# Two column pairs of a token-mixing MLP's first product as blocks of seven products, and weight sums over four steps

## The chip, the core and the metric

The kernel runs on one core of a Trainium2 chip. TensorE (PE) multiplies, with its weight loads (PEld) beside it; VectorE (DVE), ScalarE (ACT) and GpSimd (POOL) work on tiles in SBUF and on TensorE's results in PSUM; SyncE (SP) issues most of the transfers, POOL and ACT a few. All times are device microseconds. The time of the kernel is the median of several executions; the profile comes from one execution of its own.

## The reference

One sequence of 2048 tokens with 512 channels passes through a linear attention block and a token-mixing MLP, both with a residual:

```python
h  = x + A(layernorm(x), wqkv, w_phi, wo)      # linear attention, 32 heads of 16
h2 = h + B(layernorm(h), w1, b1, w2, b2)

def B(x, w1, b1, w2, b2):
    h = layernorm(x)                               # [S=2048, D=512]
    u = gelu(einsum("bsd,sf->bdf", h, w1) + b1)    # contracts the 2048 tokens, F=1792
    y = einsum("bdf,fs->bds", u, w2) + b2          # contracts F, back to 2048 tokens
    return y transposed to (tokens, channels)
```

All in float32. The change concerns B alone: its first product (w1 transposed times h) and its second (w2 transposed times u).

## The kernel before

**Arithmetic.** Each float32 operand is split into a hi part (a cast by ACT, rounded to TensorE's fast float32 format) and a lo part (the difference, by DVE or POOL); a product is the sum of three: hi·hi, hi·lo, lo·hi (`mm3`, L64 to L68; `split`, L59 to L62).

**Token loop.** After the attention's preparation (to about 136 us) a loop over `it` runs 18 times over the 16 token tiles: numerator, output projection (`s_wo`), residual `s_h` (DVE L634, with SP's store of h L635), the two layer norms' moments (`s_moments`, ACT) and `s_hn`, which leaves the normalized tile as hi and lo (`HN`, "hs"); its lo part is POOL's. The order of instructions on TensorE, DVE, ACT and POOL is written out by hand here (`manual_schedule`); SP's is left to the scheduler.

**First product.** u has 14 tiles of 128 rows (F) by 512 columns (D), taken in 7 column pairs p (`NP`). A pair sums over 16 token tiles; each contributes 2 × 3 plain products of 128×128 by 128×512 (`fill`, `mm3`: the tile name is "pu"). Pairs 0 and 1 are woven into the token loop, as the tiles appear; the others follow it. `stream` (L672 to L679) loads the weights of two token tiles by two F tiles (256 KB) and splits them: hi on ACT (L663), lo on DVE (L670). After a pair comes `gelu` (ACT, L797), which puts both tiles of u into one 128×1024 tile.

**Second product.** y has 16 tiles of tokens, taken as 8 pairs `sp`; each sums over the 7 pairs p of u: 56 steps (sp, p). A step multiplies a 2×2 block of w2 (two F tiles by two token tiles) with a 2×2 block of u (two F tiles by two halves of D, 256 columns each) in seven products instead of eight (the Strassen scheme in Winograd's form). The operands are sums of blocks: of the weights, four sums on DVE over the data of two steps at once (`w2_sums`, L848, operations of 128×256 at L854 to L857), then the seven operands are split for two steps at once (`w2_parts`, L865, 128×1792, ACT and DVE, both at L875); of u, four sums and splits once per pair (`operands_u`, L800). In `pair_of_tiles` (L933) products 1 and 6 run as `narrow` (L908): three products of 256 columns (L913). Products 2, 3, 4, 5 and 7 run as `wide` (L916): one product of 512 columns, hi·hi and hi·lo side by side (L921), and one of 256 columns for lo·hi (L924); the halves are added when the bank is read. The last pair of token tiles runs all seven as narrow, and its last three steps together: 147 products in a row. When a pair of token tiles is complete, DVE and ACT combine the banks (L972) and POOL issues three stores of 256 KB that accumulate onto h in `out` (L991, and L992 for "low"). The order is held by `in_order` (L839).

Of the kernel before, what the change touches and what calls it, by code (L numbers as in the profile page):

```python
# [31 lines left out]
LAG = 3  # L32
WARM = 10
# [4 lines left out]
def block_kernel(ctx: ExitStack, tc: tile.TileContext, x, xT, wT, phic, wo, w1, b1, w2, b2,  # L38
# [34 lines left out]
    wqp = aq.enter_context(tc.tile_pool(name="wqp", bufs=1, side="right"))  # L73
    wqh = wqp.tile([P, KD, D], F32R, name="wqh")
    wql = wqp.tile([P, KD, D], F32R, name="wql")
    kvB = wqp.tile([P, 2, P], F32, name="kvB")
    kvS = wqp.tile([P, 4, 64], F32, name="kvS")
    sums = wqp.tile([P, SUMS, NPR, 2, 2], F32, name="smq")
    wqp.tile([P, 504], F32, name="pad")
# [378 lines left out]
    ms.enter_context(tc.manual_schedule(engines={ET.PE, ET.DVE, ET.Activation, ET.Pool}))  # L458
# [112 lines left out]
    ps_f = ctx.enter_context(tc.tile_pool(name="ps_f", bufs=2, space=PSUM, reuse_waits="tile"))  # L571
    wst = ExitStack()
# [5 lines left out]
    HN, HT, PHT, OS, PO, VE = {}, {}, {}, {}, {}, {}  # L578
# [68 lines left out]
    def s_hn(t):  # L647
        hn = ak.tile([P, D], F32, name="hn")
# [23 lines left out]
    def stream(src, k0, n, c0, w):  # L672

        raw = wf.tile([P, n, w], F32, name="wraw")
        wh_ = wf.tile([P, n, w], F32R, name="whi")
        wl_ = wf.tile([P, n, w], F32R, name="wlo")
# [44 lines left out]

    for it in range(NT + 2):
# [23 lines left out]
        if it + 3 < NT:  # L746
            s_ez(it + 3)
        if 0 <= it - 2 < NT:
            s_hn(it - 2)
# [10 lines left out]
        if 0 <= it - 1 < NT:  # L760
            s_wo(it - 1)
        for w in work[1:]:
            w()
        if 0 <= it - 1 < NT:
            s_h(it - 1)
        flush(1)
    flush()
    ms.close()
    a2.close()
    aq.close()  # L770

    NP = NF // 2
    HD = D // 2
    up = ctx.enter_context(tc.tile_pool(name="up", bufs=1, side="right", reuse_waits="tile"))
    uo = ctx.enter_context(tc.tile_pool(name="uo", bufs=2, side="right", reuse_waits="tile"))
    ws = ctx.enter_context(tc.tile_pool(name="ws", bufs=2, side="right", reuse_waits="tile"))
    ur = ctx.enter_context(tc.tile_pool(name="ur", bufs=4, side="right", reuse_waits="tile"))
    ut = ctx.enter_context(tc.tile_pool(name="ut", bufs=1, side="right", reuse_waits="tile"))
    ps_b = ctx.enter_context(tc.tile_pool(name="ps_b", bufs=4, space=PSUM, reuse_waits="tile"))
    NEAR = 2
    near = [up.tile([P, 7, 2, HD], F32R, name=f"un{p}") for p in range(NEAR)]  # L790
    up.tile([P, 120], F32, name="pad")
    U, UB, far = {}, {}, {}
# [7 lines left out]
    def operands_u(p):  # L800
        u = U[p]
        tt = ut.tile([P, 3, HD], F32, name="tt")
        e = nc.gpsimd if p < NEAR else nc.vector
        e.tensor_sub(tt[:, 0], u[:, 0], u[:, 1])
        e.tensor_sub(u[:, 0], u[:, 2], u[:, 0])
        e.tensor_sub(tt[:, 1], u[:, 2], tt[:, 0])
        e.tensor_sub(tt[:, 2], u[:, 3], tt[:, 1])
        if p < NEAR:
            for n0, src in ((0, u), (4, tt)):
                o = near[p][:, n0:n0 + src.shape[1]]  # L810
                split(o[:, :, 0], o[:, :, 1], src, nc.vector)
            for m in range(7):
                UB[p, m] = near[p][:, m]
            return
        for m in range(7):
            at = (p - NEAR) * 7 + m
            if at % 2 == 0:
                far[at // 2] = big.tile([P, 2, 2, HD], F32R, name="uf", tag="big")
            UB[p, m] = far[at // 2][:, at % 2]
            split(UB[p, m][:, 0], UB[p, m][:, 1], u[:, m] if m < 4 else tt[:, m - 4], nc.vector)  # L820

    for p in range(NP):
        while FN[p] < NT:
            fill(p, ps_b)
        for c in range(2):
            gelu(2 * p + c, PU[p][c])
        if p < NEAR:
            operands_u(p)
    for p in range(NEAR, NP):
        operands_u(p)  # L830
    wst.close()
    hp = ctx.enter_context(tc.tile_pool(name="hp", bufs=1, reuse_waits="tile"))

    STEPS = [(sp, p) for sp in range(NT // 2) for p in range(NP)]
    GRP = 2
    AW, RAW = {}, {}
    QUEUE = {}

    def in_order(*ops):  # L839

        for op in ops:
            with ExitStack() as st:
                for ins in QUEUE.values():
                    st.enter_context(tc.issue_after(ins))
                ins = op().ins
            QUEUE[ins.engine] = ins

    def w2_sums(g):  # L848
        other = g > AHEAD + 2 and g % 4 == 1
        raw = RAW[g] = (hp if other else ws).tile([P, GRP, 7, P], F32, name="wraw", bufs=1 if other else 3)  # L850
        for i, (sp, p) in enumerate(STEPS[g * GRP:(g + 1) * GRP]):
            nc.sync.dma_start(raw[:, i, 0:4].rearrange("p (k i) s -> p k (i s)", k=2),
                              w2v[:, 2 * p:2 * p + 2, sp * 2 * P:(sp + 1) * 2 * P])
        sums = (lambda: nc.vector.tensor_add(raw[:, :, 4], raw[:, :, 0], raw[:, :, 2]),  # L854
                lambda: nc.vector.tensor_sub(raw[:, :, 5], raw[:, :, 4], raw[:, :, 1]),
                lambda: nc.vector.tensor_sub(raw[:, :, 0], raw[:, :, 1], raw[:, :, 0]),
                lambda: nc.vector.tensor_sub(raw[:, :, 6], raw[:, :, 3], raw[:, :, 5]))  # L857
        if g < AHEAD:
            with tc.issue_after(LO[-18]):
                for op in sums:  # L860
                    op()
        else:
            in_order(*sums)

    def w2_parts(g):  # L865
        home = hp if g % 3 == 2 else ws
        wh_ = home.tile([P, GRP, 7, P], F32R, name="whi")
        wl_ = home.tile([P, GRP, 7, P], F32R, name="wlo")
        for i, step in enumerate(STEPS[g * GRP:(g + 1) * GRP]):
            AW[step] = wh_[:, i], wl_[:, i]  # L870
        raw = RAW.pop(g)
        if g < AHEAD:
            split(wh_, wl_, raw, nc.vector)
        else:
            in_order(lambda: nc.scalar.activation(wh_, raw, AF.Copy), lambda: nc.vector.tensor_sub(wl_, raw, wh_))  # L875

    AHEAD = 2
    for g in range(AHEAD):
        w2_sums(g)
        w2_parts(g)  # L880
    for g in range(AHEAD, AHEAD + 2):
        w2_sums(g)
    parts_next, sums_next = [], []

    def stream_w2(n):

        if (n + 1) % NP == 0:
            for g in sums_next:
                w2_sums(g)
            sums_next.clear()  # L890
        if n % GRP == 0:
            parts_next.append(n // GRP + AHEAD)
        if (n + 2) % NP == 0:
            return
        for g in parts_next:
            if g * GRP < len(STEPS):
                w2_parts(g)
            if (g + 2) * GRP < len(STEPS):
                if (n + 3) % NP == 0:
                    sums_next.append(g + 2)  # L900
                else:
                    w2_sums(g + 2)
        parts_next.clear()


    P1, P2, P3, P4, P5, P6, P7 = (1, 1), (3, 3), (6, 2), (2, 6), (4, 4), (5, 5), (0, 0)

    def narrow(o, ps, m, sp, opens, closes):  # L908

        for p in ps:  # L910
            wh_, wl_ = AW[sp, p]
            for i, (x, y) in enumerate(((wh_, 0), (wh_, 1), (wl_, 0))):
                in_order(lambda: nc.tensor.matmul(o, x[:, m[0]], UB[p, m[1]][:, y], start=opens and p == 0 and i == 0,  # L913
                                                  stop=closes and p == NP - 1 and i == 2, skip_group_check=True))

    def wide(sp, p, *products):  # L916


        wh_, wl_ = AW[sp, p]
# [13 lines left out]
    def pair_of_tiles(sp, p):  # L933
# [6 lines left out]
        if t + 2 == NT:  # L940
            if p < NP - 3 or end:
# [3 lines left out]
                for o, m, opens in places if end else places[5:] + places[:5]:  # L945
                    narrow(o, ps, m, sp, opens, True)
                if end:
                    last_sums(t, HB)
# [126 lines left out]
```

## Time and profile before

| | us |
|---|---|
| median of 3 runs | 519.57 (519.33 to 519.91) |
| span of the profiled execution | 517.9 |
| TensorE busy in it | 513.2 |
| DVE, ACT, POOL busy | 395.0, 285.3, 235.9 |

The profiled execution has no time of its own beside its span; the 1.7 us between span and median are what lies around the span. By stages, from the trace's start: attention's preparation 0 to 136, token loop to 260, the five remaining column pairs to 375.5, the first seven pairs of token tiles of the second product to 496.8, the last pair with the final sums and stores to the end.

A line of a group reads: source line, engine, operation, result<-operands, shape, count | busy us, mean ns | idle time of the engine before them, and what ended it. A matmul's record has a modelled end; the distance between two starts is what one costs.

### The profile page before, as it was taken

How to read it: one execution, taken by the hardware profiler on the slowest of the kernel's cores; microseconds unless marked ns; L12 is line 12 of the kernel's file. 1: busy time of each engine (PE TensorE's matmuls, PEld its weight loads, DVE VectorE, ACT ScalarE, POOL GpSimd, SP SyncE). 2: the span in 40 equal slices, each digit the busy share in tenths (PEclk: the TensorE clock that was granted, in tenths of full speed). 3: DMA queues.
4: the chain of work that ended last, by engine and by line, in shares of the span. 5: the costliest groups of instructions: out<-in, count | busy, mean ns of one | idle time of the engine just before them, and what ended most of it. 6: DMA issues, size and time to landing. Idle time of an engine off the chain costs nothing.

```text
span 517.9 us, 9772 instructions
## 1 busy us (share of the span) xinstructions
PE 513.2 (99%) x3761; PEld 434.0 (84%) x3761; DVE 395.0 (76%) x719; ACT 285.3 (55%) x501; POOL 235.9 (46%) x182
## 2 busy tenths in 40 slices
PE   9999999999999999999999999999999999999997
PEld 8888888888887777777788888888899999999997
DVE  6799889989987899697336624625797899888993
ACT  6999853526267877767756423425464434433530
POOL 3579997876999999974224000000001102110210
PEclk9999999999999999999999999999999999999999
DMA  8642301021302334333255433532134586557732
GB/s 311 209 142 84 102 22 42 1 83 44 122 27 97 103 103 119 107 103 123 82 163 162 123 94 90 184 102 62 41 115 94 141 201 136 139 156 181 137 48 61
DMA packets 46493, 57.66 MB, mean 111 GB/s; under 512 B 4080, under 2 KB 33136, under 8 KB 46448
## 3 DMA queue, kind: packets, MB, share of 16 engines
q1 hardware_dynamic: 43136, 51.38, 31.4%
q0 software_dynamic: 3024, 5.51, 7.6%
q8 instruction: 29, 0.48, 0.4%
q10 hardware_dynamic: 288, 0.17, 0.1%
q14 instruction: 16, 0.13, 0.1%
HBM read 46.81 MB, written 10.22 MB: 110 GB/s over the span
## 4 chain that ended last, share of the span: by engine, by line
PE 97%; DVE 1%; ACT 1%; issue 0%; DVEq 0%
PE pu L66 13%; PE pu L68 12%; PE pu L67 12%; PE py L921 11%; PE py L913 10%; PE py L924 6%; PE po L66 3%; PE pk_ps L66 3%; PE po L68 3%; PE po L67 3%; PE pk_ps L67 3%; PE pk_ps L68 3%; PE pv L67 3%; PE pv L66 3%; PE pv L68 3%; PE tr L591 2%
## 5 line engine op out<-in xcount | busy, mean ns | idle before, releaser
L991 POOL DMA_DIRECT2D out<-ot x14 | 12.5, 941 | 170.3 <-DVE ot L972 170.3
L66 PE MATMUL pu<-hs,whi 128*128 128x512 f32 x224 | 87.7, 394 | 0.0
L67 PE MATMUL pu<-hs,whi 128*128 128x512 f32 x224 | 87.2, 389 | 0.0
L68 PE MATMUL pu<-hs,wlo 128*128 128x512 f32 x224 | 86.5, 389 | 0.0
L670 DVE TENSOR_TENSOR wlo<-wraw,whi 128x512 fp32r<-128x512 f32 x56 | 46.9, 841 | 46.5 <-ACT whi L663 46.2
L875 ACT ACTIVATE whi<-wraw 128x1792 fp32r<-128x1792 f32 x26 | 44.0, 1704 | 30.9 <-issue 17.4
L663 ACT ACTIVATE whi<-wraw 128x512 fp32r<-128x512 f32 x56 | 34.6, 625 | 44.4 <-PE pu L67 39.4
L875 DVE TENSOR_TENSOR wlo<-wraw,whi 128x1792 fp32r<-128x1792 f32 x26 | 52.4, 2019 | 0.0
L66 PEld LDWEIGHTS pu<-hs,whi 128*128 128x128 f32 x224 | 42.0, 188 | 9.1 <-ACT hj L641 0.2
L68 PEld LDWEIGHTS pu<-hs,wlo 128*128 128x128 f32 x224 | 42.0, 188 | 8.9
L67 PEld LDWEIGHTS pu<-hs,whi 128*128 128x128 f32 x224 | 42.1, 188 | 8.5
L921 PE MATMUL py<-uf,whi 128*128 128x512 f32 x175 | 48.4, 395 | 0.0
L484 POOL TENSOR_TENSOR ez<-eq,zB 128x1024 f32<-128x1024 f32 x16 | 38.4, 2405 | 3.8 <-ACT zB L544 3.8
L913 PE MATMUL py<-uf,whi 128*128 128x256 f32 x210 | 39.0, 283 | 0.0
L213 POOL TENSOR_TENSOR pk<-pk,sk 128x1024 f32<-128x1024 f32 x16 | 31.1, 1949 | 11.2 <-DVE sk L212 10.0
L508 POOL TENSOR_TENSOR eq<-eq,w 128x1024 f32<-128x1024 f32 x16 | 32.4, 2026 | 3.2 <-DVE w L505 3.2
L921 PEld LDWEIGHTS py<-uf,whi 128*128 128x128 f32 x175 | 30.1, 189 | 3.9
L913 PEld LDWEIGHTS py<-uf,whi 128*128 128x128 f32 x210 | 32.8, 192 | 0.0
L217 POOL TENSOR_TENSOR zacc<-zacc,pk 128x1024 f32<-128x1024 f32 x13 | 31.4, 2412 | 0.5
L924 PEld LDWEIGHTS py<-uf,wlo 128*128 128x128 f32 x175 | 27.1, 189 | 3.8
L913 PE MATMUL py<-uf,wlo 128*128 128x256 f32 x105 | 29.7, 283 | 0.0
L924 PE MATMUL py<-uf,wlo 128*128 128x256 f32 x175 | 28.7, 281 | 0.0
(200 smaller groups left out, 1303.9 us busy)
## 6 DMA issues: line engine op xcount, KB each, us to landing
wraw<-in_w SPq DMA_DIRECT2D x112, 256.0 KB, 3.0
xraw<-in_xT SPq DMA_DIRECT2D x16, 256.0 KB, 2.9
xh<-in_x SPq DMA_DIRECT2D x16, 256.0 KB, 2.6
h<-in_x SPq DMA_DIRECT2D x16, 256.0 KB, 2.7
out<-h SPq DMA_DIRECT2D x16, 256.0 KB, 2.1
out<-ot POOLq DMA_DIRECT2D x14, 256.0 KB, 4.4
wraw<-in_wT SPq DMA_DIRECT2D x12, 256.0 KB, 5.1
out<-low POOLq DMA_DIRECT2D x7, 256.0 KB, 4.2
```

What stands on the lines that cost most here:

```text
L66: nc.tensor.matmul(o, ah, bh, start=first, stop=False)
L67: nc.tensor.matmul(o, ah, bl, start=False, stop=False)
L68: return nc.tensor.matmul(o, al, bh, start=False, stop=last).ins
L217: nc.gpsimd.tensor_add(zacc, zacc, PK[t])
L484: nc.gpsimd.tensor_mul(EZ[t], EQ[t], zB)
L508: nc.gpsimd.tensor_mul(heads(EQ[t]), heads(EQ[t]), W[t].rearrange("p g c h -> p (g c h)").unsqueeze(2).to_broadcast([P, 2 * H, DH]))
L663: nc.scalar.activation(wh_, raw, AF.Copy)
L670: LO.append(nc.vector.tensor_sub(wl_, raw, wh_).ins)
L875: in_order(lambda: nc.scalar.activation(wh_, raw, AF.Copy), lambda: nc.vector.tensor_sub(wl_, raw, wh_))
L913: in_order(lambda: nc.tensor.matmul(o, x[:, m[0]], UB[p, m[1]][:, y], start=opens and p == 0 and i == 0, stop=closes and p == NP - 1 and i ...
L921: in_order(lambda: nc.tensor.matmul(o, wh_[:, m[0]], UB[p, m[1]], start=p == 0, stop=False, skip_group_check=True))
L924: in_order(lambda: nc.tensor.matmul(o[:, 0], wl_[:, m[0]], UB[p, m[1]][:, 0], start=False, stop=p == NP - 1, skip_group_check=True))
```

## The change

- **Kinds of column pairs.** Pairs 0 and 1 stay plain, inside the token loop. The other five follow `KINDS = "vuuvv"`: pair 2 plain ("v"), pairs 3 and 4 as blocks ("u"), pairs 5 and 6 plain. Their work is cut into 8 steps for each pair (a step takes two token tiles), numbered 0 to 39; the 56 steps of the second product follow as 40 to 95.
- **Block steps of the first product.** A "u" step multiplies a 2×2 block of w1 (two token tiles by two F tiles) with a 2×2 block of h (two token tiles by two halves of D) in seven products, all narrow: 21 products of 256 columns for 12 of 512. After eight steps `u_out` combines the four banks (one ACT and five DVE operations), and `u_gelu` applies gelu two steps later.
- **Operands of h.** For this the normalized float32 tiles are kept (`HF`). For each of eight pairs of token tiles four sums (`h_ops`, DVE, 128×256) and one split (`h_parts`, 128×1024) are made once and used by both block pairs. Sums of pairs 0 to 6 stand in the token loop from `it` 14 on or between the first steps, those of pair 7 behind step 3's weight parts.
- **Weights of the block steps.** SP loads 256 KB as before and one more tile of 64 KB; then POOL issues a transfer of 128 KB that adds onto the loaded tiles in SBUF (`add_raw`). Two sums by DVE for two steps remain (`w_sums`).
- **Weights of the second product.** `w_sums` makes the four sums for four steps at a time (128×512 for each operation); the splits (`w_parts`) go one step at a time (128×896, or 128×512 for a plain step) into a ring of three buffers, and for the later steps three places out of six in the pool `big`.
- **Second product.** Product 7 runs narrow in place of wide: 4 wide and 3 narrow products in a step. The signs in the combination change, and a pair of token tiles has four stores (128 KB and three of 256 KB).
- **Order.** `manual_schedule` takes SP in as well and holds to the end of the kernel; `in_order` is gone. The lo parts of the last two normalized tiles go from POOL to DVE. A Gelu on a small tile stands in iteration 10 of the token loop, and with it the table load that the first Gelu brings.

```diff
+PLAIN = 2
+KINDS = "vuuvv"
...
-    ms.enter_context(tc.manual_schedule(engines={ET.PE, ET.DVE, ET.Activation, ET.Pool}))
+    ms.enter_context(tc.manual_schedule(engines={ET.PE, ET.DVE, ET.Activation, ET.Pool, ET.SP}))
...
-        split(HN[t][:, 0], HN[t][:, 1], hn, nc.gpsimd)
+        if t < NT - 2:
+            split(HN[t][:, 0], HN[t][:, 1], hn, nc.gpsimd)
+        else:
+            nc.scalar.activation(HN[t][:, 0], hn, AF.Copy)
+            DL.append(lambda: nc.vector.tensor_sub(HN[t][:, 1], hn, HN[t][:, 0]))
...
+    def block_ops(e, v, t0, t1, t2):
+        return [lambda: e.tensor_sub(t0, v[0], v[1]), lambda: e.tensor_sub(v[0], v[2], v[0]),
+                lambda: e.tensor_sub(t1, v[2], t0), lambda: e.tensor_sub(t2, v[3], t1)]
...
+    def load_raw(g):
...
+        for k in range(2):
+            src, r, c = blocks(2 * g + k)
+            nc.sync.dma_start(RAW[g][:, k, 1:5].rearrange("p (k i) s -> p k (i s)", k=2),
+                              src[:, r:r + 2, c:c + 2 * P])
+            if STEPS[2 * g][0] == "u":
+                nc.sync.dma_start(RAW[g][:, k, 0], src[:, r + 1, c:c + P])
...
+    def add_raw(g):
...
+            nc.gpsimd.dma_start(RAW[g][:, k, 0:2].rearrange("p i s -> p (i s)"), src[:, r, c:c + 2 * P],
+                                accum_op=ALU.add)
...
+    def w_sums(g):
...
+        plain = STEPS[2 * g][0] == "y"
+        raw = BLOCK[g // 2 % 2] if plain else RAW[g]
+        if plain:
+            nc.vector.tensor_add(raw[:, :, 0], raw[:, :, 3], raw[:, :, 1])
+        nc.vector.tensor_add(raw[:, :, 5], raw[:, :, 0], raw[:, :, 2])
+        nc.vector.tensor_add(raw[:, :, 6], raw[:, :, 4], raw[:, :, 5])
+        if plain:
+            nc.vector.tensor_add(raw[:, :, 1], raw[:, :, 1], raw[:, :, 2])
+    def w_parts(n):
...
+        if n >= Y0 and (n - Y0) % 6 < 3:
+            PARTS[n] = [big.tile([P, 7, P], F32R, name="wp", tag="big") for _ in range(2)]
+        else:
+            t = ws[n % 3].tile([P, 2, 7, P], F32R, name="wp")
+            PARTS[n] = t[:, 0], t[:, 1]
+        k = slice(1, 5) if STEPS[n][0] == "v" else slice(0, 7)
+        split(PARTS[n][0][:, k], PARTS[n][1][:, k], RAW[n // 2][:, n % 2, k], nc.vector)
...
+    def h_parts(j):
+        h_sums(j)
+        v = HF.pop(j).rearrange("p i (k d) -> p (i k) d", k=2)
+        split(CB[j][:, :, 0], CB[j][:, :, 1], v, nc.vector)
...
+        if it == 10:
+            nc.scalar.activation(mhalf[:, 1:2], mhalf[:, 2:3], AF.Gelu_apprx_tanh)
...
+        some(DQ, {14: 6, 15: 6}.get(it, 0))
         if 0 <= it - 1 < NT:
             s_h(it - 1)
         flush(1)
+        some(DQ, {14: 4}.get(it, 0))
...
+    def products(n, banks, x, first, last):
+        a, b, c, d = banks
+        for o, m, opens in ((a[:, 0], P1, True), (a[:, 1], P6, False), (d[:, 0], P7, True), (b[:, 0], P5, True),
+                            (b[:, 1], P4, False), (c[:, 0], P3, True), (c[:, 1], P2, False)):
+            narrow(o, n, m, x(m[1]), first and opens, last)
...
-        w3, w2, w7, w5, w4 = (b3, P3), (b2, P2), (b7, P7), (b5, P5), (b4, P4)
...
+        w3, w2, w5, w4 = (b3, P3), (b2, P2), (b5, P5), (b4, P4)
+        if first:
+            ws_(w3, w2)
+        elif not end:
+            ws_(w3, w2, w5, w4)
+        narrow(b16[:, 0], n, P1, x(1), first, end)
+        narrow(b16[:, 1], n, P6, x(5), False, end)
+        narrow(b7[:, 0], n, P7, x(0), first, end)
...
+        if kind == "u":
+            if j == 0:
+                BANKS[0] = four_banks(i % 2)
+            products(n, BANKS[0], lambda m: NB[j][m], j == 0, j == NT // 2 - 1)
+            if j == NT // 2 - 1:
+                b = list(BANKS[0])
+                later(0, lambda: u_out(i, b))
+                later(2, lambda: u_gelu(i))
...
+    for j, n in enumerate((0, 1, 2, 3, 5, 8, 10), 1):
+        at(n - 1.5 if j > 3 else n - 0.5, h_sums, j)
+        at(n, h_parts, j)
```

More of the change, by code (lines that the diff above doesn't have):

```diff
@@ L766, in block_kernel @@
         flush(1)
-    flush()
[L768 to L792, printed above, removed]
+        some(DQ, {14: 4}.get(it, 0))
+        if it == 13:
+            for j in range(6):
+                DQ.extend(h_ops(j, nc.vector))
+        if it in (14, 15):
+            add_raw(it - 14)
+        if it == 16:
+            DQ.extend(h_ops(6, nc.vector))
+    some(DL)
+    flush()
+    U, UB, UT, SPARE = {}, {}, {}, []
     def gelu(f, pu):
@@ L822, in block_kernel @@
[L822 to L861, printed above, removed]
-        else:
-            in_order(*sums)
@@ L865, in w2_parts @@
[L865 to L875, printed above, removed]
@@ L906, in block_kernel, with u_sums @@
[L906 to L919, printed above, removed]
+    def u_sums(p):
+        u, tt = U[p], hp.tile([P, 3, HD], F32, name="tt")
+        UT[p] = tt
+        for op in block_ops(nc.vector, [u[:, k] for k in range(4)], tt[:, 0], tt[:, 1], tt[:, 2]):
+            op()
@@ new lines, in block_kernel, with narrow @@
+    for p in range(PLAIN):
+        while FN[p] < NT - 1:
+            fill(p)
+    a2.close()
+    cbb = ctx.enter_context(tc.tile_pool(name="cbb", bufs=1, side="right", reuse_waits="tile"))
+    ps_b = ctx.enter_context(tc.tile_pool(name="ps_b", bufs=4, space=PSUM, reuse_waits="tile"))
+    CB[4] = cb_tile(4)
+    P1, P2, P3, P4, P5, P6, P7 = (2, 1), (4, 3), (6, 2), (3, 6), (0, 4), (5, 5), (1, 0)
+    def narrow(o, n, m, x, opens, closes):
+        wh_, wl_ = PARTS[n]
+        for i, (w, y) in enumerate(((wh_, 0), (wh_, 1), (wl_, 0))):
+            nc.tensor.matmul(o, w[:, m[0]], x[:, y], start=opens and i == 0, stop=closes and i == 2, skip_group_check=True)
@@ L994, in last_h @@
+        if end:
+            last_sums(t, HB)
+        return []
     def last_h(t):
@@ new lines, in block_kernel @@
+    at(len(STEPS) - 18, last_h, NT - 2)
+    at(len(STEPS) - 12, last_b, NT - 2)
+    HB = []
+    load_raw(2)
+    load_raw(3)
+    load_raw(4)
+    add_raw(2)
+    step(0)
+    step(1)
+    for p in range(PLAIN):
+        fill(p)
+    step(2)
+    wst.close()
+    hp = ctx.enter_context(tc.tile_pool(name="hp", bufs=1, reuse_waits="tile"))
+    for j in range(5, NT // 2):
+        CB[j] = cb_tile(j)
+    w_parts(3)
+    load_raw(5)
+    add_raw(4)
+    made = 4
+    DQ.extend(h_ops(7, nc.vector))
@@ new lines, in block_kernel, with prepare @@
+    made = set(range(made))
+    def prepare(m):
+        if m >= len(STEPS):
+            return
+        w_parts(m)
+        made.add(m)
+        if m >= Y0:
+            if m % 4 == (2 if m > Y0 + 3 else 3):
+                w_sums(m // 4 * 2 + 2)
+        elif m % 2 == 0 and m + 2 < Y0:
+            w_sums(m // 2 + 1)
+        if m ^ 1 in made:
+            load_raw(m // 2 + 4)
+            if 2 * (m // 2 + 3) < len(STEPS):
+                add_raw(m // 2 + 3)
+    for n in range(0, len(STEPS)):
+        now[0] = n
+        ready = len(STORES)
+        if n > 2:
+            step(n)
+        if ready:
+            store()
+        for f in PENDING.pop(n - 0.5, []):
+            f()
+        if n == Y0 - 5:
+            w_sums(Y0 // 2)
+        if n + 2 < Y0 and n + 2 not in made:
+            prepare(n + 2)
+        if n + 5 >= Y0 and (n < Y0 or STEPS[n][2] != NP - 2):
+            if n > Y0 and STEPS[n][2] == NP - 1:
+                prepare(n + 4)
+            prepare(n + 5)
+        for f in PENDING.pop(n, []):
+            f()
@@ L1030, in _layout @@
+    assert not STORES
+    ms.close()
 def _layout(A_x, A_wqkv, A_w_phi, A_wo, B_w1, B_b1, B_w2, B_b2):
```

345 lines of the change are left out of this document (212 added, 133 removed).

## The prediction

> **What bounds the kernel now.** I read the busy shares first, then the chain, TensorE's waits, and only then the stages that the change touches.
>
> ```profile
> span 517.9 us, 9772 instructions
> PE 513.2 (99%) x3761; PEld 434.0 (84%) x3761; DVE 395.0 (76%) x719; ACT 285.3 (55%) x501; POOL 235.9 (46%) x182
> PEclk9999999999999999999999999999999999999999
> PE 97%; DVE 1%; ACT 1%; issue 0%; DVEq 0%
> ```
>
> TensorE is busy 99% of the span, 97% of the chain that ended last is its own work, and its granted clock is full in every slice. Its waits with a named releaser:
>
> ```profile
> PE pk_ps L352 <- DVE eps L57: 1.1, 1, 1.1
> PE pn L609 <- DVE h L634: 0.2, 1, 0.2
> ```
>
> There are 1.3 us in all, both ahead of the changed stages. So the time is a count of products times their spacing, and the other engines matter only where the change makes one of them late. The span lacks 1.7 us of the 519.57 us median; I add these to whatever span comes out.
>
> **Price of each product.** A record's duration is modelled (0.39 us), so I take distances between starts.
>
> ```profile
> 259.95 0.39 PE L66 MATMUL pu<-hs,whi 128*128 128x512 f32 x1
> ...
> 359.91 0.39 PE L66 MATMUL pu<-hs,whi 128*128 128x512 f32 x1
> ...
> 365.35 0.39 PE L66 MATMUL pu<-hs,whi 128*128 128x512 f32 x1
> ...
> 375.55 0.61 PE L921 MATMUL py<-un,whi 128*128 128x512 f32 x2
> ```
>
> The 24 products between 359.91 and 365.35 take 0.2267 us each. The 510 issued from 259.95 to 375.55 give the same 0.2267, so that whole stage has no stall.
>
> ```profile
> 379.91 0.72 PE py L913 x6
> 380.63 1.16 PE py L921 x5
> 381.79 0.59 PE py L924 x5
> 382.38 0.72 PE py L913 x6
> ...
> 496.79 17.65 PE py L913 x147
> ```
>
> In these pieces of the chain (start, length, product count) a 256-column product costs 17.65/147 = 0.120, a wide one 1.16/5 = 0.232, its 256-column low part 0.59/5 = 0.118.
>
> **TensorE's sum.** Pairs 3 and 4 lose 2 × 96 = 192 plain products: −192 × 0.2267 = −43.5 us. They become 2 × 8 steps × 21 narrow products: 336 × 0.120 = +40.3. Per pair that is 20.2 us instead of 21.8: seven eighths of the columns, at 3% more per column. In 49 steps of the second product, product 7 goes from wide plus low to three narrow ones: 3 × 0.120 − 0.232 − 0.118 = +0.01 each, +0.5. Net −2.7 us. The narrow spacing comes from a stretch of 147 in a row with the same operand shapes, each with its own weight load, so I take it unchanged (the bound above it is a rival below).
>
> The Trainium skill, "TensorE: Matmul & The Clock Gate", section "Back-to-back issue gap", would turn the sign: it gives about 131 ns for a sustained 512-column product and N/2.4 + 2.5 ns, 109 ns, for 256 columns alone. By these the sum would be −25 + 37, a loss of about 11 us. The rows above disagree by 96 ns in the wide case and decide.
>
> **DVE, the engine that must keep up.** The new work is in 128-row operations, priced by these groups (last figures: busy us, mean ns, then idle before):
>
> ```profile
> L62 DVE TENSOR_TENSOR uf<-u,uf 128x256 fp32r<-128x256 f32 x20 | 7.7, 419 | 0.3 <-ACT uf L61 0.3
> L62 DVE TENSOR_TENSOR un<-tt,un 128x768 fp32r<-128x768 f32 x2 | 1.9, 950 | 0.0
> L62 DVE TENSOR_TENSOR un<-u,un 128x1024 fp32r<-128x1024 f32 x2 | 2.7, 1340 | 2.5 <-ACT un L61 2.5
> L855 DVE TENSOR_TENSOR wraw<-wraw 128x256 f32<-128x256 f32 x28 | 11.9, 424 | 0.8
> L875 DVE TENSOR_TENSOR wlo<-wraw,whi 128x1792 fp32r<-128x1792 f32 x26 | 52.4, 2019 | 0.0
> 247.36 0.69 DVE L670 TENSOR_TENSOR wlo<-wraw,whi 128x512 fp32r<-128x512 f32 x1
> ```
>
> Thus 0.42 for 256 columns, 0.69 for 512, and on straight lines between neighbours 1.09 for 896 and 1.22 for 1024 (1.34 by the row, which I take as the upper end).
>
> The second product's weight work is not on the path. Per pair of token tiles DVE spends now 3.5 × (2.02 + 4 × 0.42) = 13.0 us on it, afterwards 7 × 1.09 + 1.75 × 4 × 0.69 = 12.5, in a TensorE time of 7 × 2.48 = 17.4. No wait of TensorE there ends with DVE before, so the sums over four steps are worth nothing; if DVE alone set the pace they would be worth at most 7 × 0.5 = 3.5 us. ACT's seven casts of 0.95 (896 columns, between its rows below) for 3.5 of 1.70 and POOL's fourth store per pair of tiles have room in the same 17.4 us, ACT being busy 52.30 of 121.30 us:
>
> ```profile
> 375.50:496.80 121.30, 121.30 (x787) 110.52 (x787) 108.74 (x192) 52.30 (x60) 15.88 (x18) 1.00 0.59 139
> ```
>
> In the token loop, iterations 14 and 15 get 16 of the h-block sums (0.42 each, 6.7 us).
>
> ```profile
> 241.10:248.00 6.90, 6.90 (x74) 5.40 (x74) 3.40 (x5) 5.04 (x12) 3.23 (x3) 1.00 0.24 76
> 248.00:254.90 6.90, 6.90 (x73) 5.39 (x72) 1.91 (x5) 4.96 (x12) 1.85 (x2) 1.00 0.24 78
> 254.90:261.70 6.80, 6.80 (x59) 5.29 (x59) 2.31 (x6) 4.90 (x11) 1.85 (x2) 1.00 0.24 77
> 240.16 1.94 POOL L508 TENSOR_TENSOR eq<-eq,w 128x1024 f32<-128x1024 f32 x1 [0.48 <-DVE w L505]
> 240.53 2.11 DVE L670 TENSOR_TENSOR wlo<-wraw,whi 128x512 fp32r<-128x512 f32 x1
> ```
>
> The windows list (after the length) busy us of TensorE, weight loads, DVE, ACT and POOL: DVE has 13.0 us free of 20.6. But a two-input DVE operation that meets POOL work lasts until POOL ends: 2.11 instead of 0.69. "SBUF — State Buffer", section "Who interferes with whom", in the Trainium skill explains it by an exclusive lock on shared ports; these two rows agree. What could be late is the h tile that TensorE transposes next. I allow 0 to 0.3 us.
>
> In iteration 16 the low parts of the plain fills' last weights, of steps 0 and 1 and of tile 14 (until now POOL's) stand in one DVE queue. ACT's part of it now:
>
> ```profile
> 257.67 0.63 ACT L61 ACTIVATE hs<-hn 128x512 fp32r<-128x512 f32 x1
> 258.21 0.62 ACT L663 ACTIVATE whi<-wraw 128x512 fp32r<-128x512 f32 x1
> ```
>
> Adding the two new casts of 0.62 and four low parts of 0.69, with DVE following ACT, the last low part ends near 261.4. TensorE wants it after six plain products from 259.95, at 261.5. Spare 0.1, so 0 to 0.5 us. Tile 15's low part, next in that queue, is wanted some 2 us after it can be there.
>
> The narrowest place is the first block pair. The part buffers are three deep, so the hi cast of step 10 waits for the end of step 7. Counted from the end of step 6: 2.72 (step 7, 12 × 0.2267) + 2 × 0.69 (pair 2's gelus ahead in ACT's queue) + 0.95 (hi, 896 columns) + 1.09 (lo) = 6.14. DVE then has, in order, two weight sums (0.84), one h part (1.22), the last four h sums (1.68) and step 11's lo (1.09): 10.97. TensorE wants that lo after 2.72 + 3 × 2.52 + 2 × 0.12 = 10.52. Late 0.45, and 0.57 at 1.34 per h part. Step 12 has no h sums ahead; the lag is not repeated. The ACT prices are:
>
> ```profile
> L875 ACT ACTIVATE whi<-wraw 128x1792 fp32r<-128x1792 f32 x26 | 44.0, 1704 | 30.9 <-issue 17.4 <-PE py L913 8.7 <-DVE wraw L857 4.8
> L797 ACT ACTIVATE u<-pu,b1s 128x512 f32<-128x512 f32 x14 | 9.5, 687 | 10.0 <-PE pu L68 9.9
> L797 ACT ACT_TABLE_LOAD x1 | 1.3, 1283 | 0.0
> 247.48 0.20 ACT L640 ACTIVATE ve<-ve 128x1 f32<-128x1 f32 x1 [1.73 <-DVE h L634]
> ```
>
> The Gelu table load, moved into the token loop, fits ACT's 1.73 us gap there: nothing; without that gap up to 1.28.
>
> Together 0 to 1.4 us of new stall, and no gain below that, as no stall stands there before. I take 0.5: the one place where the rows say late.
>
> **Transfers.**
>
> ```profile
> q1 hardware_dynamic: 43136, 51.38, 31.4%
> q0 software_dynamic: 3024, 5.51, 7.6%
> wraw<-in_w SPq DMA_DIRECT2D x112, 256.0 KB, 3.0
> out<-ot POOLq DMA_DIRECT2D x14, 256.0 KB, 4.4
> L991 POOL DMA_DIRECT2D out<-ot x14 | 12.5, 941 | 170.3 <-DVE ot L972 170.3
> ```
>
> Each block step loads 256 + 64 KB and accumulates 128 KB into them through POOL. Queue time per MB is 0.314 × 517.9/51.38 = 3.17 us, and for the 21 accumulating stores 0.076 × 517.9/21 = 1.87 us each, half for 128 KB. So a step needs 1.04 + 0.94 = 1.98 us of 2.52. Step 3 starts at 259.95 + (30 + 36) × 0.2267 = 274.9; the first accumulate is issued about then and lands (4.4 by the row) near 279.5, DVE wants it near 280; later ones are issued four steps, 10 us, ahead of their sums. Cost nothing; POOL's 0.94 us per issue hides in its idle time. As an accumulation into SBUF is not in this trace, its other end is a rival below. SP's order is now fixed too: a weight load stands behind a store of h that waits for DVE. Such a load is wanted an iteration (6.9 us) on and lands in 3.0: nothing, without that lead 3.0 once.
>
> **Forecast:** 519.57 − 2.7 + 0.5 = 517.4 us, alone 516.5 to 518.5 (no stall, less a little, to 1.6 us of it).
>
> **Rivals.**
>
> *DVE is late through the whole first block pair* (chance 0.15). From step 3's lo to step 11's, DVE has 5 × 0.69 + 4 × 1.09 + 6 × 1.22 + 12 × 0.42 + 6 × 0.42 = 22.7 us against TensorE's 5 × 2.72 + 3 × 2.52 = 21.2. For it: strided 256-column operands and POOL meetings have no row here; a fifth more is 4.5 us. Against it: DVE is through with the token loop some 7 us before step 3, though three buffers let it keep only two steps (5 us) of any lead. Of 1.5 + 4.5 us that leaves 1 to 3 us in place of the 0.5: 518.0 to 520.0, mostly no change to tell.
>
> *The accumulating loads pace the blocks* (0.11, the slower side). If their queue time is 2.5 times the row's, 0.94 → 2.35, a step takes 3.4 us: 16 × 0.87 = 14 us more, of which the 10 us between issue and sums absorb most: +4, 521 us. It decides from about 2.2 times the row, or a landing over some 13 us. For it: such a transfer reads SBUF back, unlike any load here, and POOL issues it. Against: the stores in the trace accumulate too, at 4.4 us.
>
> *The narrow products are paced by their weight loads* (0.02).
>
> ```profile
> L913 PEld LDWEIGHTS py<-uf,whi 128*128 128x128 f32 x210 | 32.8, 192 | 0.0
> ```
>
> A load lasts 0.192 us; if the loads did not overlap as they do at 0.120, 336 × 0.072 = 24 us come on top: 541. From 0.128 on the gain is gone. The page's 109 ns for 256 columns beside 131 for 512 belongs here; by its figures alone the time would be some 531.
>
> *A wait in a shared queue that I have not placed* (0.06), such as the token loop's stores ahead of SP's loads: 520 to 523.
>
> **How the numbers follow.** The forecast's case has 0.66. About 0.2%, 1 us, can be told from no change. Faster (below 518.5) takes the forecast's case and 0.02 of DVE's lateness: 0.68. Same: the other 0.13 and 0.02 of the last rival: 0.15. Slower: 0.11 + 0.02 + 0.04 = 0.17. The range begins at 516.5 (without stall 516.9, less 0.4 for spacing) and reaches to 520.0, past DVE's lateness; 0.18 or so lies outside.
>
> **What would show it.** Right: TensorE with 168 narrow products in each of two block pairs lasting 20.2 us; a stage sum 3.2 us shorter; new waits below 1.4 us, the largest on a step's lo around step 11. The first rival shows as a row of waits of narrow products for DVE over steps 9 to 15; the second as DVE weight sums waiting for POOL's transfers; the third as spacing above 0.12. Wrong in general: a wait of TensorE over 1 us anywhere from 185 us on, or a granted clock below 1.00.

## The result, and the profile after

The changed kernel takes 516.49 us (median of 4 runs, 516.23 to 517.07), the one before 519.61 (4 runs, 519.33 to 519.91): a ratio of 0.9941, 95% interval 0.9927 to 0.9955. It is 3.1 us faster where 2.2 were forecast, and 0.01 us below the lower end of the range (516.5). The page of the changed kernel, with the lines that answer to those of before:

```profile
span 514.5 us, 10292 instructions
PE 509.4 (99%) x3954; PEld 439.7 (85%) x3954; DVE 432.5 (84%) x736; ACT 300.7 (58%) x530; POOL 247.1 (48%) x195
PEclk9999999999999999999999999999999999999999
q1 hardware_dynamic: 45440, 52.43, 32.6%
q0 software_dynamic: 6336, 8.52, 12.1%
PE 95%; DVE 2%; ACT 1%; issue 0%; DVEq 0%
wraw<-in_w POOLq DMA_DIRECT2D x16, 128.0 KB, 3.9
```

TensorE is the bound as before: fewer busy us with 193 more recorded products, at a full clock. DVE has 37.5 us more to do and is still not on the path. TensorE's waits:

```profile
PE pk_ps L358 <- DVE eps L62: 1.1, 1, 1.1
PE pn L616 <- DVE h L641: 0.2, 1, 0.2
PE pu L336 <- POOL ph L361: 0.2, 1, 0.2
```

The third line is new, but this wait lies in the first 10 us, far ahead of the change. No wait stands in the first or second product. The marks between the stages, from TensorE's timeline of the changed kernel (start, length, line):

```profile
288.23 0.28 PE L951 MATMUL py<-hs,wp 128*128 128x256 f32 x1
...
328.55 0.40 PE L71 MATMUL pu<-hs,wp 128*128 128x512 f32 x1
...
372.09 0.39 PE L958 MATMUL py<-cb,wp 128*128 128x512 f32 x1
...
493.19 0.28 PE L951 MATMUL py<-cb,wp 128*128 128x256 f32 x1
```

The block pairs take 328.55 − 288.23 = 40.32 us for 336 narrow products: 0.1200 each. The second product's first 49 steps take 493.19 − 372.09 = 121.10; read at the same places before they take 121.08.

To see where a span differs I cut each trace at four products: the 41st, the last of the output projection, the first of the second product, the first of the last 147. The differences of their starts, in us, for the profiled executions of all kernels below:

| kernel | to the 41st | token loop | first product | second product | rest | span |
|---|---|---|---|---|---|---|
| before | 7.92 | 251.80 | 115.83 | 121.08 | 21.29 | 517.91 |
| after | 7.41 | 252.01 | 112.67 | 121.10 | 21.26 | 514.45 |
| x1_plain | 7.59 | 252.13 | 115.83 | 121.10 | 21.25 | 517.91 |
| x2_sums_late | 8.23 | 252.03 | 115.23 | 121.52 | 21.46 | 518.46 |
| x3_dve_sums | 7.47 | 252.04 | 113.31 | 121.10 | 21.25 | 515.17 |
| x4_two_steps | 7.46 | 252.04 | 112.71 | 121.10 | 21.25 | 514.55 |
| x5_three | 7.88 | 251.96 | 114.09 | 127.43 | 21.55 | 522.90 |
| x6_pool_lo | 7.69 | 252.02 | 112.65 | 121.10 | 21.26 | 514.71 |
| x7_table | 7.47 | 251.80 | 112.67 | 121.81 | 21.56 | 515.31 |
| x7_again | 7.77 | 251.79 | 112.65 | 121.10 | 21.26 | 514.58 |
| x8_sums_ahead | 7.61 | 252.01 | 112.66 | 121.10 | 21.25 | 514.63 |
| x9_seven_wide | 7.50 | 252.49 | 112.66 | 121.32 | 21.27 | 515.24 |
| c0_after | 8.48 | 252.02 | 112.70 | 121.68 | 21.26 | 516.13 |

Between before and after, 3.16 of the 3.46 us come from the first product. 0.51 more come from the start, which varies between executions (the rows of after and c0_after, 7.41 and 8.48, are the same kernel), and 0.21 are lost in the token loop.

### The profile page after: what moved, and what is told of

Same layout as the page of the kernel before. It is cut to its first block, busy times and chain, and to the rows that moved or that the text cites. A ratio compares the mean times of both kernels' runs of the same rounds, so it can differ in the third digit from the quotient of the medians.

```text
span 514.5 us, 10292 instructions
## 1 busy us (share of the span) xinstructions
PE 509.4 (99%) x3954; PEld 439.7 (85%) x3954; DVE 432.5 (84%) x736; ACT 300.7 (58%) x530; POOL 247.1 (48%) x195
## 3 DMA queue, kind: packets, MB, share of 16 engines
q0 software_dynamic: 6336, 8.52, 12.1%
## 4 chain that ended last, share of the span: by engine, by line
PE 95%; DVE 2%; ACT 1%; issue 0%; DVEq 0%
PE py L951 22%; PE pu L71 10%; PE pu L72 9%; PE pu L73 9%; PE py L958 9%; PE py L960 4%; PE pk_ps L71 3%; PE pk_ps L72 3%; PE pk_ps L73 3%; PE pv L73 3%; PE pv L72 3%; PE pv L71 3%; PE po L71 3%; PE po L73 2%; PE po L72 2%; PE pn L616 2%
## 5 line engine op out<-in xcount | busy, mean ns | idle before, releaser
L66 ACT ACTIVATE wp<-wraw 128x896 fp32r<-128x896 f32 (+1 forms) x96 | 79.8, 869 | 83.4 <-DVE wraw L797 34.1
L67 DVE TENSOR_TENSOR wp<-wraw,wp 128x896 fp32r<-128x896 f32 (+1 forms) x96 | 92.3, 986 | 20.7 <-ACT wp L66 20.5
L951 PE MATMUL py<-cb,wp 128*128 128x256 f32 x582 | 79.8, 283 | 0.0
L951 PEld LDWEIGHTS py<-cb,wp 128*128 128x128 f32 x582 | 74.0, 191 | 0.0
L71 PE MATMUL pu<-hs,wp 128*128 128x512 f32 x96 | 37.4, 389 | 0.0
L72 PE MATMUL pu<-hs,wp 128*128 128x512 f32 x96 | 37.4, 389 | 0.0
L73 PE MATMUL pu<-hs,wp 128*128 128x512 f32 x96 | 37.3, 389 | 0.0
L958 PE MATMUL py<-cb,wp 128*128 128x512 f32 x126 | 36.1, 394 | 0.0
L951 PE MATMUL py<-uf,wp 128*128 128x256 f32 x198 | 26.6, 283 | 0.0
L71 PE MATMUL pu<-wq,xs 128*128 128x512 f32 x64 | 26.1, 408 | 0.0
L71 PE MATMUL pu<-hs,whl 128*128 128x512 f32 x64 | 26.0, 406 | 0.0
L71 PE MATMUL po<-woh,oh 128*128 128x512 f32 x64 | 25.3, 395 | 0.1
L72 PE MATMUL pu<-wq,xs 128*128 128x512 f32 x64 | 25.0, 391 | 0.0
L72 PE MATMUL pu<-hs,whl 128*128 128x512 f32 x64 | 25.0, 390 | 0.0
```

Source lines behind the costliest of these rows:

```text
L66: nc.scalar.activation(hi, src, AF.Copy)
L67: lo_engine.tensor_sub(lo, src, hi)
L71: nc.tensor.matmul(o, ah, bh, start=first, stop=False)
L72: nc.tensor.matmul(o, ah, bl, start=False, stop=False)
L73: return nc.tensor.matmul(o, al, bh, start=False, stop=last).ins
L951: nc.tensor.matmul(o, w[:, m[0]], x[:, y], start=opens and i == 0, stop=closes and i == 2, skip_group_check=True)
```

## The experiments

**x1_plain: no block steps.**

```diff
-KINDS = "vuuvv"
+KINDS = "vvvvv"
-            PU[i] = [{2: ps_b, 5: ps_f, 6: ps_q}[i]...
+            PU[i] = [{2: ps_b, 3: ps_f, 4: ps_q, 5: ps_f, 6: ps_q}[i]...
-all calls of h_ops, h_parts and h_sums
```

> All five later column pairs plain (no block steps, no sums or splits of h, no accumulating loads); order, second product and its weight sums stay as changed. Theory (the gain is the TensorE sum of the block steps and nothing else): 192 x 0.2268 - 336 x 0.120 = 3.2 us more than the changed kernel, 519.7 us, no wait of TensorE in the first product, the second product still 121.1 us for its first 49 steps. Rival (part of the gain comes from the new order or the second product): 517 to 518.5 us.

Measured: 519.96 us (11 runs; against before 1.0008, 0.9999 to 1.0017). The first product takes 115.83 us, as before to the hundredth, and the other stages stay as in the changed kernel. Without the block steps the gain is gone, and the stage that they change is 115.83 − 112.67 = 3.16 us longer: they are the whole gain.

**x2_sums_late and x8_sums_ahead: the sums of h out of the token loop.** Both drop the calls that put 16 sums into iterations 14 and 15; the second also reorders what is left.

```diff
 # both
-        some(DQ, {14: 6, 15: 6}.get(it, 0))
-        some(DQ, {14: 4}.get(it, 0))
 # x8_sums_ahead
-            some(DQ, 4)
+            some(DQ, 8)
-        at(n - 1.5 if j > 3 else n - 0.5, h_sums, j)
+        at(n - 0.5, h_sums, j + 1)
```

> The 16 sums of h that stood in iterations 14 and 15 of the token loop come just ahead of their splits instead, between steps 0 and 3 (some 7 us more for DVE there). Theory (DVE's idle time between 264 and 288 us, 6.4 us, takes nearly all of it): 516.5 to 517.5 us, a wait of TensorE below 1 us. Rival (DVE in order is late through the whole first block pair): 518.5 to 520.5 us with waits on the low parts of steps 9 to 15.

Measured: 520.32 us (10 runs, ratio 1.0011, 1.0002 to 1.0020): the gain is gone, and my theory with it. The rival's time came out, but not its mechanism: there is one wait, in step 4, and none in the first block pair. TensorE's timeline of x2_sums_late, with the wait in brackets, then DVE's and ACT's:

```profile
278.40 0.39 PE L72 MATMUL pu<-hs,wp 128*128 128x512 f32 x1
281.07 0.50 PE L73 MATMUL pu<-hs,wp 128*128 128x512 f32 x1 [2.28 <-DVE wp L67]
```

```profile
271.69 1.23 DVE L67 TENSOR_TENSOR cb<-u,cb 128x1024 fp32r<-128x1024 f32 x1 [1.13 <-ACT cb L66]
272.83 0.88 DVE L738 TENSOR_TENSOR u<-u 128x256 f32<-128x256 f32 x2
273.74 0.89 DVE L739 TENSOR_TENSOR u<-u 128x256 f32<-128x256 f32 x2
275.76 1.23 DVE L67 TENSOR_TENSOR cb<-u,cb 128x1024 fp32r<-128x1024 f32 x1 [1.13 <-ACT cb L66]
...
280.33 0.68 DVE L67 TENSOR_TENSOR wp<-wraw,wp 128x512 fp32r<-128x512 f32 x1
```

```profile
270.60 1.06 ACT L66 ACTIVATE cb<-u 128x1024 fp32r<-128x1024 f32 x1 [2.47 <-DVE u L739]
274.66 1.06 ACT L66 ACTIVATE cb<-u 128x1024 fp32r<-128x1024 f32 x1 [3.00 <-DVE u L739]
275.63 0.61 ACT L66 ACTIVATE wp<-wraw 128x512 fp32r<-128x512 f32 x1
278.73 1.06 ACT L66 ACTIVATE cb<-u 128x1024 fp32r<-128x1024 f32 x1 [2.49 <-DVE u L739]
```

The two queues wait for each other in turn: four sums on DVE (1.8), the cast on ACT (1.06, DVE idle 1.13), the low part on DVE, the next four sums (ACT idle 2.5 to 3.0). The cast of step 4's weights stands in ACT's queue behind the second of these casts, its low part on DVE behind more sums; it ends at 281.01, and TensorE starts the product that needs it at 281.07. DVE was not full over this stretch: it idled 1.13 us in each turn, and was full only from 275.76 on, when it was behind. Whether order or volume is the cause is what x8 asks.

> As x2_sums_late (no sums of h in the token loop), but the four sums of the next pair of tiles stand ahead of each split, not those of the same pair. Theory (the wait of x2_sums_late comes from two queues in order that wait for each other: sums on DVE, cast on ACT, low part on DVE, with the next weights' cast behind it, not from DVE's volume): with the sums done early the wait falls from 2.4 to below 0.8 us, 516.5 to 517.7 us. Rival (7 us more for DVE are too much for that stretch): a wait of 2 us or more remains, 519 us and more.

Measured: 517.21 us (4 runs, 516.41 to 517.28; ratio 0.9952, 0.9937 to 0.9966), and in its trace no wait of TensorE behind the token loop, the first product in 112.66 us. The same sums, again out of iterations 14 and 15, cost nothing in the first product once each stands one pair ahead of the cast that needs it. So it is the order of two in-order queues, not their load.

**x3_dve_sums: no accumulating loads.**

```diff
     def add_raw(g):
-        if STEPS[2 * g][0] != "u":
-            return
+        return
-            if STEPS[2 * g][0] == "u":
-                nc.sync.dma_start(RAW[g][:, k, 0], src[:, r + 1, c:c + P])
-        plain = STEPS[2 * g][0] == "y"
-        raw = BLOCK[g // 2 % 2] if plain else RAW[g]
+        plain = True
+        raw = BLOCK[g // 2 % 2] if STEPS[2 * g][0] == "y" else RAW[g]
```

> No accumulating loads and no 64 KB loads: DVE makes all four weight sums of the block steps (two more of 128x256 for two steps). Theory (the transfers cost nothing, DVE has 0.29 us to spare at step 11's low part): two sums of 0.42 more ahead of it make TensorE wait some 0.5 us there and nowhere else: 517.0 us. Rival (the accumulating transfers, POOL's issues of them or their blocking of DVE cost time that now comes back): 516.0 us or less. Second rival (DVE needs the relief throughout): 518 us and more with waits at many steps.

Measured: 517.18 us (5 runs, ratio 0.9953, 0.9940 to 0.9965), and one wait, in step 11, on its low part:

```profile
296.65 0.39 PE L948 MATMUL py<-hs,wp 128*128 128x256 f32 x1 [0.40 <-DVE wp L67]
```

The product before it starts at 295.97, so the distance is 0.68 in place of 0.12: 0.56 us, and the first product is 113.31 − 112.67 = 0.64 us longer. The accumulating loads cost nothing and save this much.

**x4_two_steps: weight sums of the second product over two steps.**

```diff
-        raw = BLOCK[g // 2 % 2] if plain else RAW[g]
+        for raw in [RAW[g], RAW[g + 1]] if plain else [RAW[g]]:
```

> The weight sums of the second product for two steps at a time again (twice as many operations, of 128x256, in the same places). Theory (DVE is off the path there): DVE 8 us busier in the second product, 115.5 of 121.1, the least spare time of a low part falls from 2.0 to about 0.5 us, no wait of TensorE: 516.5 us, within 0.3. Rival (the grouping is what lets DVE keep up beside the new split sizes): waits in the second product, 518 to 520 us.

Measured: 516.37 us (4 runs, ratio 0.9939, 0.9926 to 0.9953), no wait. The windows of the second product, changed kernel and x4_two_steps (length, then busy us of TensorE, its weight loads, DVE, ACT, POOL):

```profile
372.10:493.20 121.10, 121.10 (x835) 112.57 (x834) 107.46 (x160) 55.60 (x87) 21.00 (x24) 1.00 0.66 146
```

```profile
372.20:493.20 121.00, 121.00 (x834) 112.48 (x833) 109.18 (x204) 54.52 (x86) 20.99 (x24) 1.00 0.65 146
```

The windows differ by 1.7 us of DVE, but they cut off different operations at their ends. All 112 sums together, against 56 of twice the size, last 8.6 us longer in this trace, as expected; DVE's busy time over the whole span grows by 5.1 us (437.6 for 432.5), as operations back to back overlap. TensorE does not notice: the weight sums over four steps are worth nothing on the path.

**x5_three: a third block pair.**

```diff
-KINDS = "vuuvv"
+KINDS = "vuuuv"
-    U_WORK = {0: 20, 1: 22, 2: 25, 3: 27, 4: 30, 5: 34, 6: 41}
+    U_WORK = {0: 28, 1: 30, 2: 32, 3: 34, 4: 36, 5: 38, 6: 41}
-            PU[i] = [{2: ps_b, 5: ps_f, 6: ps_q}[i]...
+            PU[i] = [{2: ps_b, 6: ps_b}[i]...
```

> Three block pairs (3, 4, 5) and two plain ones; the sums and splits of u for the second product stand up to eight steps later, as the tiles that they go into hold the operands of h until then. By TensorE's sum alone 1.6 us less than the changed kernel: 514.9 us. Theory (DVE is then the bound): from step 24 to 39 DVE gets some 50 us of work in 42 us, so 3 to 6 us of waits on low parts in steps 28 to 46: 518 to 521 us. Rival (its lead and the second product's idle time absorb it): 515 to 516 us.

Measured: 524.87 us (4 runs, ratio 1.0102, 1.0087 to 1.0117), worse than my range. Its waits, and windows around the start of the second product (the last columns are the granted clock, the DMA share and GB/s):

```profile
PE py L958 <- ACT u L911: 3.6, 1, 3.6
PE pu L73 <- DVE wp L67: 2.1, 3, 0.8
```

```profile
330.00:360.00 30.00, 30.00 (x209) 28.14 (x208) 27.65 (x46) 18.01 (x25) 0.00 (x0) 1.00 0.35 102
360.00:380.00 20.00, 14.28 (x63) 10.70 (x61) 19.31 (x35) 10.78 (x20) 0.00 (x0) 0.95 0.31 103
380.00:384.70 4.70, 4.70 (x17) 4.16 (x17) 4.63 (x8) 3.52 (x7) 0.00 (x0) 0.50 0.33 112
```

DVE is busy 27.65 of 30 us and then 19.31 of 20: here it is the bound. The last Gelu stands in ACT's queue behind casts that wait for DVE, and TensorE's first product of the second stage waits 3.6 us for it. In the last of these windows the granted clock is 0.50. DVE's volume was foreseen, the half clock was not. Three block pairs were not tuned further.

**x6_pool_lo and x7_table: two moves that I had costed.** The first puts the low parts of the last two normalized tiles back on POOL, the second takes the small Gelu out of the token loop.

```diff
 # x6_pool_lo
-        if t < NT - 2:
+        if True:
 # x7_table, x7_again
-        if it == 10:
-            nc.scalar.activation(mhalf[:, 1:2], mhalf[:, 2:3], AF.Gelu_apprx_tanh)
```

> The low parts of the last two normalized tiles on POOL again, as before the change. Theory (DVE has only 0.2 us to spare at tile 14's low part, and one POOL operation of 1.29 us blocks it or is blocked by it): TensorE waits 0.3 to 1 us at the end of the token loop or ahead of step 2: 516.8 to 517.5 us. Rival (POOL's 1.29 us run beside DVE's queue): no wait, 516.5 us.

Measured: 516.63 us (4 runs), no wait at the end of the loop; the rival was right, and this move is worth nothing.

> Without the small Gelu in the token loop: the table load comes with the first real Gelu again, behind step 3. Theory (ACT's casts have over 4 us to spare there, as they had 1.7 us in the loop): no wait in either place, 516.5 us, within 0.4. Rival (the 1.28 us matter in one of the two places): 1 us more if the loop hid it and step 3 doesn't, up to 0.3 us less if the loop did not hide it.

Measured: 516.25 us (4 runs, 516.03 to 517.08). Loop 251.80 in place of 252.01, first product unchanged. Its second product shows 0.7 us that no theory had, so I ran it again beside the unchanged copy of the changed kernel:

> x7_table with more rounds, beside the changed kernel. Theory (the table load in the token loop costs 0.2 us on the path, and nothing behind step 3): the loop 251.8 us instead of 252.0, first product the same 112.7; 0.2 us less than the changed kernel, if the loads of the second product don't hide it. Rival (the 0.2 us was the one execution's): the same loop time as in the changed kernel.

> The changed kernel once more, beside x7_again. 516.5 us within 0.4; in its trace the token loop takes 252.0 us from the 41st product to its last one, as in the profile that is there, and the first product 112.7 us.

Measured: x7_again 516.35 (5 runs, 516.08 to 516.78; ratio 0.9938, 0.9926 to 0.9951), c0_after 517.05 (5 runs, 516.19 to 517.91; 0.9950, 0.9937 to 0.9962). The loop's 0.2 us sits at one product of the output projection. TensorE's timeline, first c0_after, then x7_again:

```profile
228.76 0.39 PE L73 MATMUL pu<-hs,whl 128*128 128x512 f32 x1
229.27 0.50 PE L71 MATMUL po<-woh,oh 128*128 128x512 f32 x1
```

```profile
228.05 0.39 PE L73 MATMUL pu<-hs,whl 128*128 128x512 f32 x1
228.34 0.50 PE L71 MATMUL po<-woh,oh 128*128 128x512 f32 x1
```

0.51 against 0.29. By the loop's stage x7_table is 0.2 us faster than the changed kernel, in both of its profiles; the intervals of the medians overlap and the spans differ by more for other reasons, so the times alone don't show it.

**x9_seven_wide: product 7 wide again.**

```diff
-            ws_(w3, w2, w5, w4)
+            ws_(w3, w2, w7, w5, w4)
-        narrow(b7[:, 0], n, P7, x(0), first, end)
...
         sub(u3, u2, b7[:, 0])
+        sub(u3, u3, b7[:, 1])
```

> Product 7 of the second product wide again (5 wide and 2 narrow in a step, one sum more for a pair of token tiles). By the prices of the prediction 49 x 0.01 = 0.5 us less: the first 49 steps in 120.6 us. Rival (narrow products behind others cost 0.118 and not 0.120, as the trace of the changed kernel has it): no difference, 121.1 us.

Measured in one execution, 517.01 us: the 49 steps take 121.32 us, of which gaps at 391.8 and 443.5 us are about 0.25; without them they take about 121.1. That is not 120.6: the rival's time holds, with the reservation that it is a single execution. (The 0.5 us more of its token loop lie just behind the 41st product, ahead of 8 us, where the edit changes nothing.)

## Why the prediction was right, and where it was not

**The bound and the main term: right.** The block pairs' narrow products came out at 0.1200 us and the plain ones beside them at 0.227. The forecast +40.3 − 43.5 = −3.2 was measured as −3.16, and x1 gives it back in full. The rival of the weight loads did not occur. One figure in the prediction beside this term is wrong: a narrow product costs 6% more per column than a plain one, not 3% (0.1200/256 against 0.2267/512 us); the sums use the spacings and don't change. The figures of the Trainium skill, "TensorE: Matmul & The Clock Gate", section "Back-to-back issue gap" (about 131 ns sustained for 512 columns, 109 by its formula for 256 alone), would by the prediction's estimate have made it a loss; here 227 and 120 ns were measured.

**Product 7: mis-sized.** The +0.5 was 49 times 0.01, a difference of two rounded prices. The chain of the changed kernel, in its first steps with all parts:

```profile
374.72 0.92 PE py L958 x4
375.64 0.47 PE py L960 x4
376.11 1.08 PE py L951 x9
377.19 0.93 PE py L958 x4
```

A step is 377.19 − 374.72 = 2.47 us, what it was. The term measured +0.02.

**Stalls in the block pair: the right place, the wrong sign.** I put the narrowest place at step 11's low part, late by 0.45. DVE's timeline of the changed kernel:

```profile
290.00 1.09 DVE L67 TENSOR_TENSOR wp<-wraw,wp 128x896 fp32r<-128x896 f32 x1 [1.29 <-ACT wp L66]
291.00 0.42 DVE L794 TENSOR_TENSOR wraw<-wraw 128x256 f32<-128x256 f32 x1
291.46 0.43 DVE L795 TENSOR_TENSOR wraw<-wraw 128x256 f32<-128x256 f32 x1
291.80 1.22 DVE L67 TENSOR_TENSOR cb<-hf,cb 128x1024 fp32r<-128x1024 f32 x1
292.94 0.88 DVE L738 TENSOR_TENSOR hf<-hf 128x256 f32<-128x256 f32 x2
293.85 0.89 DVE L739 TENSOR_TENSOR hf<-hf 128x256 f32<-128x256 f32 x2
294.65 2.09 DVE L67 TENSOR_TENSOR wp<-wraw,wp 128x896 fp32r<-128x896 f32 x2
```

The order is the one in the sum. ACT's timeline at the same place:

```profile
287.75 1.37 ACT L911 ACTIVATE u<-pu,b1s 128x512 f32<-128x512 f32 x2 [1.04 <-PE pu L73]
289.02 0.94 ACT L66 ACTIVATE wp<-wraw 128x896 fp32r<-128x896 f32 x1
```

The low part of step 10 ends at 291.09, 5.58 after the end of step 6 (285.51) where I had 6.14: ACT takes the first Gelu at 287.75, half a us before the end of step 7 (288.23), as its tile is complete by then. From there to step 11's low part (start 294.65, 1.09 long, so 295.74) it is 4.65 where I had 4.83, as neighbours overlap. Together 0.74 earlier: 0.29 to spare. It is the narrowest place that was found in the block pairs: x3 put two more sums in front, and the wait came there and nowhere else.

**Sums in the token loop: right for a reason only half seen.** I allowed 0 to 0.3 us and there was no wait. But I had weighed DVE's idle time only. x2 shows the cover's price, 2.6 us, and x8 that the order between DVE and ACT makes it.

**The table load: wrong.** I had it hidden in ACT's gap of 1.73 us. That gap was read from another iteration, at 247 us. The Gelu stands at 216 us, and there the trace of the kernel before has a gap of 0.17 ahead of the moments. It costs 0.21 us in the loop, and nothing behind step 3, where it was: the three profiles without it in the loop take 251.79 to 251.81 us there, all with it 251.96 or more. The traces show how the delay travels; first c0_after, then x7_again, which runs 0.70 us ahead of it at this place:

```profile
215.92 1.28 ACT L888 ACT_TABLE_LOAD   x1
218.77 0.55 POOL L652 TENSOR_TENSOR r<-ve,mhalf 128x1 f32<-128x1 f32 x1 [0.18 <-PE pn L616]
219.98 2.27 DVE L684 TENSOR_TENSOR whl<-wraw,whl 128x512 fp32r<-128x512 f32 x1
```

```profile
217.85 0.55 POOL L652 TENSOR_TENSOR r<-ve,mhalf 128x1 f32<-128x1 f32 x1
219.28 2.03 DVE L684 TENSOR_TENSOR whl<-wraw,whl 128x512 fp32r<-128x512 f32 x1
```

ACT's moments end late, POOL's next operation, which needs them, starts 0.92 − 0.70 = 0.22 late (the profile names TensorE's L616 for its wait; in x7_again L652 starts ahead of that one's end, so it is not the cause), and so does the long POOL operation behind it (2.4 us). DVE's low part meets that one and lasts 2.27 in place of 2.03. DVE carries the 0.2 us in its queue to L625, for which the delayed product of TensorE waits in these traces. (Such a low part does not quite last until POOL ends, as the prediction has it: here it ends 0.55 us behind POOL's 221.70.)

**The end of the loop and the transfers: right.** No wait at tile 14, with or without the move (x6). The accumulating loads landed in 3.9 us (the line of the page above), and neither TensorE nor a weight sum of DVE in the block pairs waited for them. Queue q0 took 0.121 × 514.5 = 62.3 us for 8.52 MB. If its stores (6.42 MB) cost the 7.14 us per MB of before, the 16 loads took 16.4 us: an estimate of 1.0 us each, near the 0.94 of the prediction and far from the rival's 2.35.

**What the sum did not have.** The start, −0.51 in this pair of profiles, is chance: two executions of one kernel differ by more. The second product was forecast without a cost and has a small, unsteady one: in c0_after

```profile
472.61 0.69 DVE L793 TENSOR_TENSOR wraw<-wraw 128x512 f32<-128x512 f32 x1 [2.44 <-DMA wraw<-in_w]
...
477.52 0.42 DVE L1040 TENSOR_TENSOR u<-py,u 128x256 f32<-128x256 f32 x1
```

DVE waits 2.44 us for a weight load, and the reading of a bank behind it in the queue comes late enough to cost TensorE 0.58 us (121.68 for 121.10). x7_table loses 0.71 at the same place and x2_sums_late 0.42; the profiled execution of the changed kernel shows the same wait with a shorter length, and no loss:

```profile
469.68 0.69 DVE L793 TENSOR_TENSOR wraw<-wraw 128x512 f32<-128x512 f32 x1 [0.61 <-DMA wraw<-in_w]
```

Why such a load is late in some executions stays open; it was not tried.

Put together in the span: −2.2 forecast, −0.48 (product 7), −0.5 (no stall), −0.51 (start), +0.21 (table load), −3.5 by these terms and −3.46 measured. So the mechanism and the main term were right; that the time lies at the lower edge of the range comes from two terms of +0.5 that were not there, and on which side of 516.5 it falls is chance, as the medians of the changed kernel are 516.49 and 517.05.

## What to carry to other kernels

Where one engine is busy 99% of the span, count its operations and multiply by start-to-start distances taken from a long run of the same shape: that gave the main term within 0.05 us. For the engines that feed it, walk their queues in order, not their totals: in x2 DVE idled twice shortly before TensorE had to wait for it, since two queues waited for each other in turn, and putting the producer one item ahead removed the wait. And operations back to back overlap in these traces, so a sum of durations comes out too long; the distances of starts are what to add.

## What the runs showed of the hardware

In x5 TensorE waits 3.6 us, from 375.86 to 379.48. Its granted clock is 0.97 on average from 376 to 378, 0.50 from there to 384.7 and full behind that. So it fell about 2.0 us after the last product's modelled end, and came back 5.2 us after the wait. In between, products of 256 columns started 0.213 us apart, not 0.120, so the wait cost more than its length. In the profiled execution of x2 a wait of 2.28 us left the clock full, and the products were back at 0.23 from the second one on. But five of the ten executions of x2 have a mean granted clock of 0.995 to 0.997, where the other five have 1.0 and those of the kernel before 0.999 or 1.0. So waits of this length seem to cost some clock in some executions; where it was lost in them was not traced.

The Trainium skill, "TensorE: Matmul & The Clock Gate", section "What's actually happening", has the array fall to half its clock after an idle window of some 3.4 us and come back after a busy one of that order. The half clock and the slow return in x5 agree; the fall came sooner, after about 2.0 us without a product, and here the measurement decides.

Two executions of the same kernel differ by 1.07 us before their 41st product (7.41 and 8.48), and all nine runs of it by 1.72 us (516.19 to 517.91). For differences of tenths the stages of a trace tell more than the medians.
